# One store over 128 partitions in place of two over 64, in an attention and SoLU kernel

## The chip, the cores and the metric

The kernel runs on one core of one Trainium2 chip. The metric is the device time of one launch in microseconds; smaller is better. The core has five engines with a queue of instructions each: PE (TensorE, matrix products), ACT (ScalarE), DVE (VectorE), POOL (GpSimd) and SP (SyncE, which here only issues DMAs and waits). A DMA is issued by an engine's queue and carried out by the core's 16 DMA engines, which this document calls streams.

## What is computed

The reference, cut to what matters, takes q, k and v of shape (8, 8, 576, 64): eight batches, eight heads, 576 positions.

```python
kv  = np.einsum('bhsd,bhse->bhde', k, v)
o   = np.einsum('bhsd,bhde->bhse', q, kv)
x   = o / np.sqrt(np.mean(o * o, axis=-1, keepdims=True) + 1e-06) * g_norm   # heads side by side: 4608 x 512
h   = x @ w_in                                     # 4608 x 1024
solu = h * softmax(h)
ln  = (solu - mean(solu)) / np.sqrt(var(solu) + 1e-06) * g_ln
out = ln @ w_out                                   # 4608 x 512, float32
```

The result has 4608 rows of 512 float32 numbers, 9.44 MB.

## The kernel before

The 4608 rows are worked on in nine chunks of 512 rows. A position s of a batch is split as s = 9p + j, with p from 0 to 63 and j from 0 to 8. Chunk c of the first eight holds the positions with j from 0 to 7 of batch c; chunk 8 holds the positions with j = 8 of all eight batches.

For each chunk PE forms kv and o, ACT and DVE normalise o to x, PE forms h, ACT takes its exponential, DVE multiplies the two to u, and statistics of u give a factor `rstd` for each row. PE then forms u @ w_out, four tiles m = 0 to 3 of 128 rows into PSUM (`out_mm`, L608; its matmuls are line 612). For chunks 4 to 8 (`TOKEN_ROWS`) u has the rows on the partitions, and must be turned first: `u_turn` (L517) issues one DMA transpose for each m on SP's queue (line 519), and `out_mm` of that m waits for it. The q of chunks 5 to 8 (`Q_BY_DMA`) is turned by DMA on SP's queue too (`q_turn`, L301, line 304), and the chunk's o waits for that.

`scale` (L618) multiplies a PSUM tile by `rstd` into an SBUF tile `ob`. In chunks 0 to 7 two scaled tiles, m = yh and m = yh + 2, share one `ob` tile of 128 partitions by 2 x 512 numbers. `store_pair` (L634) then writes it out. On partition 64x + p stand the rows j = 2(2yh + x) and the next of position group p, and these are next to each other in memory: 1024 numbers, 4096 bytes. So each half of the partitions (x = 0, x = 1) goes with one DMA of 64 pieces of 4 KB, 256 KB in all, line 637. All sixteen of these pairs go by SP's queue. In chunk 8 a tile m holds two batches, 64 rows each; `store` (L645) writes each batch with one DMA of 64 pieces of 2 KB (line 647; m = 1 and 2 on ACT's queue, m = 0 on SP's). Its last tile, m = 3, is cut into two halves of 256 columns (`out_cols`, L649, matmuls on line 653; `scale_cols`, L655), and `store_cols` (L663) writes each with two DMAs of 64 pieces of 1 KB, line 666, the first half on SP's queue and the second on ACT's.

The order of all 844 pieces of work is written out by hand in `TABLE`, in one list for all engines; an engine takes its own pieces in that order and waits where an operand is not there. The same table gives each tile its place in memory, and places of `ob` tiles are used again by later tiles once the store has read them. Read from the table, SP issues from its first store on, with S(c, yh) for a pair of stores, uT(c, m) for a turn of u and qT(c) for a turn of q:

S(1,0), S(2,0), qT(5), qT(7), S(1,1), qT(6), uT(4,0), uT(4,3), uT(4,1), qT(8), S(3,0), S(3,1), uT(4,2), uT(5,0), uT(5,1), S(4,1), uT(5,3), uT(5,2), S(2,1), uT(6,0), uT(6,1), S(0,1), S(4,0), uT(6,2), uT(6,3), S(0,0), uT(7,0), uT(7,2), uT(7,1), S(5,1), uT(7,3), uT(8,1), S(6,1), S(5,0), uT(8,2), uT(8,0), uT(8,3), S(6,0), S(7,1), S(7,0), then the first tile and the first half-tile of chunk 8.

A turn of u moves 128 x 1024 two-byte numbers, 256 KB. The inputs are loaded by POOL's queue.

Of the kernel before, what the change touches and what calls it, by code (L numbers as in the profile page):

```python
# [102 lines left out]
def kernel(  # L103
# [11 lines left out]
    nc = tc.nc  # L115
    B, H, S, D = q.shape
    n_tok, d_model = out.shape
# [4 lines left out]
    NC = B + 1  # L122
# [7 lines left out]
    T = {}  # L130
# [144 lines left out]
    def kv_copy(engine, b, g, x, part):  # L275
        t = T["P", "kv", b, g, x]
        if b < 2:
            copy(engine, kvd[:, b, x, g], t[:, :, :])
        elif part == 0:
            copy(engine, kvd[:, b, x, x], t[:, :, :])  # L280
        else:
            z = part - 1
            copy(engine, kvd[z * 64:z * 64 + 64, b, 1 - x, x], t[(1 - z) * 64:(1 - z) * 64 + 64, :, :])
# [84 lines left out]
    for c in range(NC):  # L368
        if c < B:
            for g in halves(c):  # L370
                plan.add(("kv_mm", c, g), "pe", lambda _, c=c, g=g: kv_mm(c, g), [("k", c, g), ("v", c, g)],
                         uses=[("L", "k", c), ("L", "v", c)], first=[("P", "kv", c, g, x) for x in range(2)])
                for x in range(2):
                    for part in range(1 if c < 2 else 3):
                        plan.add(("kv", c, g, x, part), ("dve", "act"),
                                 lambda e, c=c, g=g, x=x, part=part: kv_copy(e, c, g, x, part),
# [5 lines left out]
        for hf in range(2):  # L382
            mine = [loads[hf]] if c < 2 else loads
            qT, qT_key = (("qT", c), ("L", "qT", c)) if c in Q_BY_DMA else (("qT", c, hf), ("S", "qT", c, hf))
            if c not in Q_BY_DMA:
                plan.add(("qT_mm", c, hf), "pe", lambda _, c=c, hf=hf: qT_mm(c, hf), ["ident", *mine], uses=quse,
                         first=[("P", "qT", c, hf)])
# [6 lines left out]
            for z in range(2):  # L394
                i = (c, hf, z)
                plan.add(("sq", i), "act", lambda _, i=i: o_sq(*i), [("o_mm", c, hf)], uses=[("P", "o", *i)],
                         first=[("S", "osq", *i)])
                plan.add(("s_mm", i), "pe", lambda _, i=i: s_mm(*i), [("sq", i)], uses=[("S", "osq", *i)],
                         first=[("P", "s", *i)])
                if c == 0:  # L400
                    plan.add(("ex", i), "act", lambda _, i=i: s_rsqrt(*i), [("s_mm", i)], uses=[("P", "s", *i)],
                             first=[("S", "rst", *i)])
                else:
                    plan.add(("ln", i), "act", lambda _, i=i: s_ln(*i), [("s_mm", i), "table"], uses=[("P", "s", *i)],
                             first=[("S", "lss", *i)])
                    plan.add(("ex", i), "act", lambda _, i=i: s_exp(*i), [("ln", i)], uses=[("S", "lss", *i)],
                             first=[("S", "rst", *i)])
                plan.add(("x", i), "dve", lambda _, i=i: x_mul(*i), [("ex", i)], after=[("x", (c, hf, 0))] if z else [],
                         uses=[("P", "o", *i), ("S", "rst", *i)] + ([("S", "x", c, hf)] if z else []),
                         first=[] if z else [("S", "x", c, hf)])  # L410
# [126 lines left out]
    for c in range(NC):  # L537
        xs = [[("x", (c, hf, z)) for z in range(2)] for hf in range(2)]
        if c not in TOKEN_ROWS:
            for f in range(NF):  # L540
                n_parts = h_parts(c)
                for part in range(n_parts):
# [4 lines left out]
                             first=[] if part else [("P", "h", c, f)],  # L547
# [5 lines left out]
                         first=[] if f % 2 else [("S", "u", c, f // 2)])  # L553
# [3 lines left out]
                         first=[] if f % 2 else [("S", "usq", c, f // 2)])  # L557
                if f % 2:
                    n = f // 2
# [3 lines left out]
                             first=[] if n % 2 else [("S", "es", c, n // 2)])  # L563
            for part, kind in enumerate(("u", "usq", "es")):
# [4 lines left out]
                         first=[] if part else [("P", "sum", c)])  # L569
            plan.add(("stats", c), "dve", lambda _, c=c: stats(c), [("sums", c, 2)], uses=[("P", "sum", c)])  # L570
        else:
            for m in range(4):
                for s in range(2):
# [7 lines left out]
                             first=[] if s else [("S", "u", c, m)])  # L581
# [33 lines left out]
    def paired(c):  # L615
        return c < B
# [15 lines left out]
    QUEUES = {"sp": nc.sync, "act": nc.scalar, "pool": nc.gpsimd}  # L632

    def store_pair(engine, c, yh):  # L634
        for x in range(2):
            j = 2 * (2 * yh + x)
            QUEUES[engine].dma_start(
                out[c * S:c * S + S, :].rearrange("(p j) d -> p (j d)", j=9)[:, j * d_model:(j + 2) * d_model],
                T["L", "ob", c, yh][64 * x:64 * x + 64].rearrange("p z d -> p (z d)"),
            )  # L640

    def rows_of(z, y):
        return out.rearrange("(b p j) d -> j b p d", p=64, j=9)[8, 2 * y + z]

    def store(engine, c, m):  # L645
        for x in range(2):
            QUEUES[engine].dma_start(rows_of(m // 2, 2 * (m % 2) + x), T["S", "ob", c, m][64 * x:64 * x + 64, :])  # L647

    def out_cols(x):  # L649
        cols = slice(x * d_model // 2, (x + 1) * d_model // 2)  # L650
# [11 lines left out]

    def store_cols(x):  # L663
        cols = slice(x * d_model // 2, (x + 1) * d_model // 2)
        for y in range(2):
            (nc.sync, nc.scalar)[x].dma_start(
                rows_of(1, 2 + y)[:, cols], T["S", "ob", NC - 1, 3, x][64 * y:64 * y + 64, :]
            )

    for half in range(2):  # L670
        plan.add(("w_mean", half), "pe", lambda _, half=half: w_mean(half), [("w_out", half), "g_mean"], after=[("w_mean", 0)] if half else [],
# [3 lines left out]
    for c in range(NC):  # L675
        last = c == NC - 1
        if c in TOKEN_ROWS:
            u_need = lambda m, half, c=c: [("uT", c, m)]
            u_use = lambda m, c=c: [("S", "uT", c, m)]
        else:  # L680
            u_need = lambda m, half, c=c: [("u", c, f) for f in range(4 * half, 4 * half + 4)]
            u_use = lambda m, c=c: [("S", "u", c, n) for n in range(NF // 2)]
        for m in range(3 if last else 4):
            for half in range(2):
                plan.add(("out", c, m, half), "pe", lambda _, c=c, m=m, half=half: out_mm(c, m, half),
                         [("w_center", f) for f in range(4 * half, 4 * half + 4)] + u_need(m, half), after=[("out", c, m, 0)] if half else [],
                         uses=u_use(m) + ([("P", "acc", c, m)] if half else []), first=[] if half else [("P", "acc", c, m)])
            plan.add(("ob", c, m), ("dve", "act"), lambda e, c=c, m=m: scale(e, c, m), [("out", c, m, 1), ("rstd", c)],
                     uses=[("P", "acc", c, m)] + ([("L", "ob", c, m % 2)] if paired(c) and m > 1 else []),
                     first=[("S", "ob", c, m)] if not paired(c) else [] if m > 1 else [("L", "ob", c, m)],  # L690
                     after=[("ob", c, m - 2)] if paired(c) and m > 1 else [])
            if last:
                plan.add(("store", c, m), ("sp", "act"), lambda e, c=c, m=m: store(e, c, m), [("ob", c, m)], uses=[("S", "ob", c, m)])
            elif m > 1:
                plan.add(("store", c, m - 2), "sp", lambda e, c=c, m=m: store_pair(e, c, m - 2),
                         [("ob", c, m), ("ob", c, m - 2)], uses=[("L", "ob", c, m - 2)])
        for x in range(2 if last else 0):
            plan.add(("out", c, 3, x), "pe", lambda _, x=x: out_cols(x),
                     [("w_center", f) for f in range(NF)] + u_need(3, 0) + u_need(3, 1), uses=u_use(3),
                     first=[("P", "acc", c, 3, x)])  # L700
            plan.add(("ob", c, 3, x), ("dve", "act")[x], lambda _, x=x: scale_cols(x), [("out", c, 3, x), ("rstd", c)],
                     uses=[("P", "acc", c, 3, x)], first=[("S", "ob", c, 3, x)])
            plan.add(("store", c, 3, x), ("sp", "act")[x], lambda _, x=x: store_cols(x), [("ob", c, 3, x)],
                     uses=[("S", "ob", c, 3, x)])
# [32 lines left out]
```

## Time and profile before

| What | Value |
|---|---|
| time, median of 3 runs | 186.5 us (186.12 to 187.28) |
| profiled execution, its own time | 186.57 us |
| its span, first to last instruction | 184.8 us |
| PE busy | 169.9 us, 92% of the span |
| ACT, DVE, POOL busy | 138.4, 123.2, 70.7 us |
| bytes moved by DMA | 34.60 MB, of these 9.44 MB written to memory |
| queue q1 (SP's DMAs) | 33264 packets, 16.33 MB |
| queue q0 (POOL's loads) | 15936 packets, 17.30 MB |
| queue q10 (ACT's DMAs) | 480 packets, 0.66 MB |

The time is 1.8 us more than the span, and the profiled execution lies 0.07 us above the median. A view of DMAs gives for each queue the packets, the megabytes, and the time that the packets took as a share of 16 streams. Its issue lines give how many DMAs a line issued, the size of one, and the median time from issue to landing. The view of stretches of time (windows) gives each engine's busy time with the number of instructions, the granted PE clock, the DMA share of 16 streams and the GB/s. A row of the timeline has start, duration, engine, line, operation, tiles and count; an engine with a q behind its name issues DMAs.

### The profile page before, as it was taken

What the parts mean: (1) busy time and instruction counts of PE and PEld (TensorE: products, weight loads), DVE (VectorE), ACT (ScalarE), POOL (GpSimd) and SP (SyncE); (2) the same over time, 40 slices, a digit from 0 to 9 for tenths busy, and PEclk for the clock granted to TensorE, in tenths of its full rate; (3) what the DMA queues carried; (4) which work ended last, traced back from release to release, by engine and by line L of the source; (5) the groups of instructions that cost most, each with busy time, mean ns of one, the idle gap of its engine ahead of it and who ended that gap; (6) DMA issues with size and microseconds to landing.
All of it is one profiled execution on the core that took longest, in us unless ns stands there. A gap on an engine that the chain in (4) does not pass through costs nothing.

```text
span 184.8 us, 4941 instructions
## 1 busy us (share of the span) xinstructions
PE 169.9 (92%) x1959; PEld 83.7 (45%) x1981; DVE 123.2 (67%) x294; ACT 138.4 (75%) x327; POOL 70.7 (38%) x105
## 2 busy tenths in 40 slices
PE   7979599979999999999999999999999999999950
PEld 2445344545445545464554444445444444344430
DVE  1011857798666675478666998888779978869430
ACT  2045878967798768986858999998899888877410
POOL 7953028697999068657950000001100300102000
PEclk9999999999999999999999999999999999999995
DMA  3999999999999999999799785650999966889975
GB/s 43 183 206 203 207 280 291 167 188 196 202 199 207 211 204 248 222 203 204 137 242 230 155 173 125 164 114 14 196 194 246 153 170 32 206 183 244 249 238 163
DMA packets 49703, 34.60 MB, mean 187 GB/s; under 512 B 32648, under 2 KB 46224, under 8 KB 49680
## 3 DMA queue, kind: packets, MB, share of 16 engines
q0 software_dynamic: 15936, 17.30, 54.3%
q1 hardware_dynamic: 33264, 16.33, 40.3%
q10 hardware_dynamic: 480, 0.66, 1.2%
q8 instruction: 15, 0.25, 0.5%
q14 instruction: 8, 0.07, 0.1%
HBM read 32.51 MB, written 9.44 MB: 227 GB/s over the span
## 4 chain that ended last, share of the span: by engine, by line
PE 73%; DMA 11%; ACT 7%; issue 2%; ACTq 2%; POOL 2%; DVE 0%; DVEq 0%; POOLq 0%
PE acc_ps L612 30%; PE h_ps L487 16%; PE h_ps L421 11%; DMA k_sb<-in_k_dram 8%; PE s_ps L341 4%; PE kv_ps L270 4%; PE o_ps L327 3%; DMA uT_sb<-u_sb 3%; PE sum_ps L459 2%; ACT osq_sb L176 2%; PE warm_ps L204 2%; ACT rst_sb L176 2%; ACTq L647 2%; PE qT_ps L293 1%; ACT e_sb L176 1%
## 5 line engine op out<-in xcount | busy, mean ns | idle before, releaser
L176 ACT ACTIVATE e_sb<-h_ps 128x512 f32<-128x512 f32 x72 | 42.1, 599 | 6.6 <-PE h_ps L421 3.1
L487 PE MATMUL h_ps<-w_in_sb,x_sb 128*128 128x512 bf16 x156 | 37.3, 379 | 0.3 <-issue 0.2
L612 PE MATMUL acc_ps<-w_out_sb,uT_sb 128*128 128x512 bf16 x147 | 35.9, 379 | 0.6 <-DMA uT_sb<-u_sb 0.3
L363 DVE SCALAR_TENSOR_TENSOR x_sb<-o_ps,g_rep,rst_sb 128x512 bf16<-128x512 f32 x36 | 26.0, 747 | 11.5 <-ACT rst_sb L176 11.2
L504 DVE SCALAR_TENSOR_TENSOR u_sb<-h_ps,e_sb 128x512 bf16<-128x512 f32 x40 | 26.9, 687 | 7.3 <-ACT e_sb L176 7.1
L612 PE MATMUL acc_ps<-w_out_sb,u_sb 128*128 128x512 bf16 x123 | 30.8, 379 | 0.2
L421 PE MATMUL h_ps<-x_sb,w_in_sb 128*128 128x512 bf16 x123 | 29.9, 379 | 0.4 <-issue 0.2
L447 POOL TENSOR_TENSOR es_sb<-e_sb 128x512 bf16<-128x512 f32 x16 | 20.3, 1275 | 21.1 <-ACT e_sb L176 18.6
L436 DVE TENSOR_TENSOR u_sb<-h_ps,e_sb 128x512 bf16<-128x512 f32 x32 | 21.3, 685 | 9.5 <-ACT e_sb L176 9.2
L525 POOL TENSOR_TENSOR both<-su 128x4 f32<-128x4 f32 x4 | 1.7, 422 | 65.6 <-DVE u_sb L504 65.6
L176 ACT ACTIVATE osq_sb<-o_ps 128x512 bf16<-128x512 f32 x36 | 20.6, 601 | 4.7 <-PE o_ps L327 4.6
L487 PEld LDWEIGHTS <-x_sb 128*128 128x128 bf16 x160 | 15.3, 98 | 18.4 <-issue 0.6
L176 ACT ACTIVATE lss_sb<-s_ps 128x512 f32<-128x512 f32 x32 | 19.1, 606 | 4.9 <-PE s_ps L341 4.5
L612 PEld LDWEIGHTS <-uT_sb 128*128 128x128 bf16 x152 | 14.5, 98 | 17.9 <-DMA uT_sb<-u_sb 0.8
L630 DVE TENSOR_SCALAR ob_sb<-acc_ps,rstd 128x512 f32<-128x512 f32 x22 | 16.2, 746 | 5.9 <-PE acc_ps L612 4.2
L176 ACT ACTIVATE rst_sb<-lss_sb 128x512 f32<-128x512 f32 x32 | 19.7, 636 | 0.3
L421 PEld LDWEIGHTS <-w_in_sb 128*128 128x128 bf16 x128 | 11.9, 98 | 14.6 <-issue 1.8
L612 PEld LDWEIGHTS <-u_sb 128*128 128x128 bf16 x128 | 12.1, 98 | 14.3 <-DVE x_sb L363 0.3
L443 POOL TENSOR_TENSOR usq_sb<-u_sb 128x512 bf16<-128x512 bf16 x15 | 15.6, 1043 | 4.1 <-DVE u_sb L436 4.1
L515 DVE SCALAR_TENSOR_TENSOR e_sb<-u_sb 128x512 f32<-128x512 bf16 x25 | 16.9, 688 | 0.2
L341 PE MATMUL s_ps<-osq_sb,head_mean 128*128 128x512 bf16 x36 | 13.3, 379 | 2.4 <-ACT osq_sb L176 2.3
L176 ACT ACTIVATE ob_sb<-acc_ps,rstd 128x512 f32<-128x512 f32 (+1 forms) x14 | 9.4, 675 | 5.7 <-DMA out_dram<-ob_sb 5.6
(80 smaller groups left out, 186.0 us busy)
## 6 DMA issues: line engine op xcount, KB each, us to landing
out_dram<-ob_sb SPq DMA_DIRECT2D x32, 256.0 KB, 3.7
q_sb<-in_q_dram POOLq DMA_DIRECT2D x6, 576.0 KB, 11.8
v_sb<-in_v_dram POOLq DMA_DIRECT2D x6, 576.0 KB, 11.5
k_sb<-in_k_dram POOLq DMA_DIRECT2D x6, 576.0 KB, 10.8
w_out_f<-in_moe_w_out_dram POOLq DMA_DIRECT2D x2, 1024.0 KB, 10.1
v_sb<-in_v_dram POOLq DMA_DIRECT2D x4, 288.0 KB, 8.2
k_sb<-in_k_dram POOLq DMA_DIRECT2D x4, 288.0 KB, 8.9
q_sb<-in_q_dram POOLq DMA_DIRECT2D x4, 256.0 KB, 9.0
```

Of the source, the lines that this page charges most:

```text
L176: nc.scalar.activation(out=dst, in_=src, func=func, **more)
L341: nc.tensor.matmul(t[:, :], head_mean[:, :], T[("S", "osq", *i)][:, :], start=True, stop=True)
L363: nc.vector.scalar_tensor_tensor(out=dst, in0=T["P", "o", c, hf, z].rearrange("p a b c -> p a (b c)"), scalar=g_rep[:, :], in1=T["S", "rst ...
L421: nc.tensor.matmul(T["P", "h", c, f][:, :], w_in_sb[:, dt, f * 128:(f + 1) * 128], flat(T["S", "x", c, dt // 2][:, dt % 2]), start=(dt == ...
L436: nc.vector.tensor_tensor(out=half_of("u", c, f), in0=T["P", "h", c, f][:, :], in1=T["S", "e", c, f][:, :], op=MUL)
L443: nc.gpsimd.tensor_tensor(out=dst, in0=src, in1=src, op=MUL)
L447: (nc.gpsimd if engine == "pool" else nc.vector).tensor_tensor(out=dst, in0=T["S", "e", c, 2 * n][:, :], in1=T["S", "e", c, 2 * n + 1][:, ...
L487: nc.tensor.matmul(t[:, :], T["S", "x", c, dt // 2][:, dt % 2, z, y:y + 2, :].rearrange("p y c -> p (y c)"), w_in_sb[:, dt, 512 * s:512 * ...
L504: nc.vector.scalar_tensor_tensor(out=T["S", "u", c, m][:, s, :], in0=T["P", "h", c, m, s][:, :], scalar=1.0, in1=T["S", "e", c, m, s][:, : ...
L515: nc.vector.scalar_tensor_tensor(out=dst, in0=src, scalar=1.0, in1=src, op0=MUL, op1=MUL, accum_out=acc)
L612: nc.tensor.matmul(T["P", "acc", c, m][:, :], u_cols(c, m, f), w_out_sb[:, f, :], start=(f == 0), stop=(f == NF - 1))
L630: nc.vector.tensor_scalar_mul(out=dst, in0=src, scalar1=by)
```

## The change

Each `ob` tile of 128 partitions is written by one DMA in place of two over 64 partitions each. The destination is written as a pattern of two blocks (step 4096 bytes within the row group for a pair, two batches for chunk 8) of 64 pieces; the source is the whole tile. The pieces keep their sizes of 4, 2 and 1 KB, the queues and the table stay as they are. SP then issues 16 pair stores in place of 32, and chunk 8 has five stores in place of ten.

```diff
     def store_pair(engine, c, yh):
-        for x in range(2):
-            j = 2 * (2 * yh + x)
-            QUEUES[engine].dma_start(
-                out[c * S:c * S + S, :].rearrange("(p j) d -> p (j d)", j=9)[:, j * d_model:(j + 2) * d_model],
-                T["L", "ob", c, yh][64 * x:64 * x + 64].rearrange("p z d -> p (z d)"),
-            )
-
-    def rows_of(z, y):
-        return out.rearrange("(b p j) d -> j b p d", p=64, j=9)[8, 2 * y + z]
+        QUEUES[engine].dma_start(
+            out[c * S:c * S + S, :].rearrange("(p j) d -> p (j d)", j=9)[:, 4 * yh * d_model:4 * (yh + 1) * d_model]
+            .rearrange("p (y n) -> y p n", y=2),
+            T["L", "ob", c, yh].rearrange("p z d -> p (z d)"),
+        )
+
+
+    def last_rows(m):
+        first = 4 * (m % 2) + m // 2
+        return out.rearrange("(b p j) d -> j b p d", p=64, j=9)[8, first:first + 3:2]
 
     def store(engine, c, m):
-        for x in range(2):
-            QUEUES[engine].dma_start(rows_of(m // 2, 2 * (m % 2) + x), T["S", "ob", c, m][64 * x:64 * x + 64, :])
+        QUEUES[engine].dma_start(last_rows(m), T["S", "ob", c, m][:, :])
...
     def store_cols(x):
         cols = slice(x * d_model // 2, (x + 1) * d_model // 2)
-        for y in range(2):
-            (nc.sync, nc.scalar)[x].dma_start(
-                rows_of(1, 2 + y)[:, cols], T["S", "ob", NC - 1, 3, x][64 * y:64 * y + 64, :]
-            )
+        (nc.sync, nc.scalar)[x].dma_start(last_rows(3)[:, :, cols], T["S", "ob", NC - 1, 3, x][:, :])
```

## The prediction

> **What bounds the kernel now.** I read the page's chain of work first, then the issue lines of the DMA view, then the DMA view of short stretches, and last SP's timeline.
>
> ```profile
> span 184.8 us, 4941 instructions
> PE 73%; DMA 11%; ACT 7%; issue 2%; ACTq 2%; POOL 2%; DVE 0%; DVEq 0%; POOLq 0%
> ```
>
> PE carries the end: 73% of the chain. DMA has 11% of it. The stores are off it until the last microseconds; what PE does wait for is turned data that comes through the same queue as the stores. So the stores are free only as long as they do not hold up the turns behind them on SP's queue.
>
> ```profile
> out_dram<-ob_sb SPq DMA_DIRECT2D x32, 256.0 KB, 3.7
> ...
> uT_sb<-u_sb SPq DMA_TRANSPOSE x20, 3.1
> ...
> out_dram<-ob_sb SPq DMA_DIRECT2D x2, 64.0 KB, 2.2
> ...
> g_rows<-in_moe_g_ln_dram SPq DMA_DIRECT2D x1, 4.0 KB
> ```
>
> A store of 256 KB lands in 3.7 us, a turn of u in 3.1 us. The reader should notice the last row: the load of `g_rows` (8 rows of 512 bytes, line 151) is the one group without a time to landing, and the view prints that time only when it counts 16 completions for each DMA. The DMA view of two stretches shows why. First, 4.6 to 6.5 us, where only the `g_rows` load runs on q1; then 148.0 to 150.4 us, where q1 moves the two halves of S(0,0).
>
> ```profile
> q1 hardware_dynamic: 16, 0.00, 1.3%
> ```
>
> ```profile
> q1 hardware_dynamic: 160, 0.52, 84.8%
> ```
>
> The load of 8 rows made 16 packets: 8 of data, and so 8 for completion. The two stores of 64 pieces made 160: 128 of data, and so 16 for completion each. A completion packet comes from each stream that takes part. So the number of streams is not always 16: it was 8 for a pattern whose slowest count is 8, and 16 for one whose slowest count is 64.
>
> **The change, part by part.** *Streams.* This decides everything. The tile side of the new store still counts 128 partitions slowest, but the memory side now counts 2 blocks slowest, then 64 pieces. If both sides are cut along their slowest count, as the 8-row load suggests, there are 2 equal parts, and 2 streams carry the whole store. The trace of before has no DMA whose memory side alone starts with so small a count, so it does not show this. Bounds: 16 streams (nothing changes but the issues) and 2 streams. I take 2, because the 8-row load is the nearest row in kind: it is the only small slowest count, and it held its DMA to that count.
>
> The Trainium skill's page "DMA: Bandwidth & Descriptors", section "Why a DMA increments its semaphore by 16 and not by 1", states that the number of engines is the largest one up to 16 that divides the slowest non-1 count of both sides, on this path the lowest-numbered ones. By that, the sum is the one below; the 8 completions of `g_rows` agree with it, and no run here yet shows it for a memory side of 2.
>
> *One pair store.* It moves 512 KB, so 262,144 bytes by each of 2 streams. What a stream moves is read from the view of stretches as GB/s over 16 times the share. The first row is the stretch in which streams moved most, the second one in which all were full of stores:
>
> ```profile
> 174.90:175.20 0.30, 0.30 (x3) 0.18 (x2) 0.30 (x2) 0.00 (x0) 0.00 (x0) 1.00 0.99 396
> 148.00:149.00 1.00, 1.00 (x6) 0.49 (x5) 0.95 (x3) 1.00 (x4) 0.00 (x0) 1.00 0.98 201
> ```
>
> 396 / (0.99 x 16) = 25.0 GB/s, so 10.5 us for a pair; 201 / (0.98 x 16) = 12.8 GB/s, so 20.5 us. I take 25.0, since two busy streams press on memory far less than 16; 12.8 stays as the upper bound. The same 25.0 GB/s gives 131,072 / 25.0 = 5.2 us for a tile of chunk 8 and 2.6 us for a half-tile.
>
> *What stands behind it.* A turn also goes through SP's queue and uses all streams, these two among them, so a turn behind a store waits for it. Its own share of the queue I take as the time of its issue: 1.26 us for a turn of u, 3.27 us for qT(5) to qT(7), 1.82 us for qT(8).
>
> ```profile
> L519 SPq DMA_TRANSPOSE uT_sb<-u_sb x20: 1231/1260/2462, 102.4 to 170.0; - x20
> ```
>
> ```profile
> L304 SPq DMA_TRANSPOSE qT_sb<-q_sb x3: 2072/3272/3489, 90.7 to 97.6; - x3
> L304 SPq DMA_TRANSPOSE qT_sb<-q_last x1: 1817/1817/1817, 106.5 to 106.5; - x1
> ```
>
> SP's timeline of before gives the order; a row joins neighbours of one kind:
>
> ```profile
> 68.68 21.79 SPq L637 DMA_DIRECT2D out_dram<-ob_sb  x4
> 90.70 5.53 SPq L304 DMA_TRANSPOSE qT_sb<-q_sb  x2
> 96.33 1.18 SPq L637 DMA_DIRECT2D out_dram<-ob_sb  x2
> 97.61 3.49 SPq L304 DMA_TRANSPOSE qT_sb<-q_sb  x1
> 102.42 3.94 SPq L519 DMA_TRANSPOSE uT_sb<-u_sb  x3
> 106.53 1.82 SPq L304 DMA_TRANSPOSE qT_sb<-q_last  x1
> 111.74 2.95 SPq L637 DMA_DIRECT2D out_dram<-ob_sb  x4
> 114.78 8.55 SPq L519 DMA_TRANSPOSE uT_sb<-u_sb  x3
> 128.09 1.11 SPq L637 DMA_DIRECT2D out_dram<-ob_sb  x2
> 129.29 3.73 SPq L519 DMA_TRANSPOSE uT_sb<-u_sb  x2
> 133.08 1.22 SPq L637 DMA_DIRECT2D out_dram<-ob_sb  x2
> 134.54 3.63 SPq L519 DMA_TRANSPOSE uT_sb<-u_sb  x2
> 138.22 3.09 SPq L637 DMA_DIRECT2D out_dram<-ob_sb  x4
> 141.41 5.31 SPq L519 DMA_TRANSPOSE uT_sb<-u_sb  x2
> 146.77 1.23 SPq L637 DMA_DIRECT2D out_dram<-ob_sb  x2
> 149.95 8.05 SPq L519 DMA_TRANSPOSE uT_sb<-u_sb  x3
> 158.05 1.23 SPq L637 DMA_DIRECT2D out_dram<-ob_sb  x2
> 160.29 2.91 SPq L519 DMA_TRANSPOSE uT_sb<-u_sb  x2
> 163.74 2.65 SPq L637 DMA_DIRECT2D out_dram<-ob_sb  x4
> 167.25 4.02 SPq L519 DMA_TRANSPOSE uT_sb<-u_sb  x3
> 171.36 8.08 SPq L637 DMA_DIRECT2D out_dram<-ob_sb  x6
> 179.54 1.38 SPq L647 DMA_DIRECT2D out_dram<-ob_sb  x2
> 181.01 1.23 SPq L666 DMA_DIRECT2D out_dram<-ob_sb  x2
> ```
>
> S(1,0), issued at 68.7 us, costs nothing even at 20.5 us: the next DMA of this queue, S(2,0), goes out just ahead of 90.5 us (68.68 + 21.79). If that cover were gone, the walk would start up to 10.5 us later. From 90.5 us I walk the two streams: S(2,0) to 101.0; qT(5) and qT(7) to 107.5; S(1,1) to 118.0; qT(6) to 121.3, which before was issued at 97.6, so PE now waits for o of chunk 6 some 18 us; three turns of u to 125.1; qT(8) to 126.9; S(3,0) and S(3,1) to 147.9; uT(4,2) to 149.2. Here is the one place where the queue runs dry by my reading: S(4,1) needs the product of chunk 4 that waits for uT(4,2). Before, uT(4,2) went out at 114.8, landed about 3.1 us later (117.9), and S(4,1) followed at 128.1, 10.2 us after. So S(4,1) starts at 159.4, and uT(5,0) and uT(5,1) fill only 2.5 of these 10.2 us: 7.7 us idle. Elsewhere what the next DMA needs is made while the queue is still busy: the turn that it rests on lies at least one store, 10.5 us, earlier.
>
> On from 159.4: S(4,1) 169.9, two turns 172.4, S(2,1) 182.9, two turns 185.4, S(0,1) and S(4,0) 206.4, two turns 208.9, S(0,0) 219.4, three turns 223.2, S(5,1) 233.7, two turns 236.2, S(6,1) and S(5,0) 257.2, three turns 261.0, S(6,0), S(7,1) and S(7,0) 292.5. Then chunk 8: three tiles, 15.7 us, and two half-tiles, 5.2 us, to 313.4. ACT's queue issues three of these five, but onto the same two streams, so they add up all the same. As a sum: 90.5 + 15 x 10.5 + 11.6 (four turns of q) + 20 x 1.26 + 7.7 + 20.9 = 313.4. About 2 us to the end of the span (a 64 KB store lands in 2.2 us), and the 1.8 us by which the profiled execution's 186.57 us exceeds its span: 317 us. That execution stands at the median, so nothing is added for it.
>
> *Issues.* 21 stores instead of 42 are issued, saving SP and ACT about half a microsecond for each (1.11 us for the two at 128.09); that is hidden behind the streams and I cost it at nothing. *Places of `ob`.* A store lands some 8 us later, so a later `ob` tile in its place waits (ob(3,0) uses that of S(2,0)); the queue is full by more than that, so nothing is added.
>
> **The rivals.** *A, not slower:* the 128 partitions decide alone, and 16 streams run as before. Then only issues go, which counts at the end:
>
> ```profile
> 175.29 3.06 ACTq L647 DMA_DIRECT2D out_dram<-ob_sb  x4
> ...
> 178.46 0.47 ACT L176 ACTIVATE ob_sb<-acc_ps,rstd 128x256 f32<-128x256 f32 x1 [5.59 <-DMA out_dram<-ob_sb]
> 178.96 1.71 ACTq L666 DMA_DIRECT2D out_dram<-ob_sb  x2
> ```
>
> ACT issues four stores for 3.06 us ahead of its last scale, and two after it for 1.71. With half of them, up to 1.5 + 0.9 = 2.4 us go, less what PE then holds back: about 2 us, 184.5 us. It decides if a store leaves 16 completion packets. For it: 64 and 128 both divide by 16, and nothing measured has a small count on the memory side alone. Against it: the 8-row load.
>
> The Trainium skill speaks for A as well: the same page, section "Rules for kernel authors", advises one 128-partition transfer instead of two over disjoint halves, as these share the engines anyway. By that alone the sum would be A's 184.5 us. The two halves of S(0,0) on q1 above agree that both use 16 streams.
>
> *B:* 2 streams, but another pair for each store. Then stores overlap one another and the turns are held up by one store at most; what remains is the tail, where a half-tile takes 2.6 us instead of a fraction, and a turn late by up to 10.5 us once or twice: about 200 us. For it speaks nothing in the trace, against it nothing either.
>
> *C:* 2 streams, the same pair, but turns do not stand behind stores. Then the streams still carry all stores: 313.4 - 36.8 (turns) - 7.7 = 268.9, plus 3.8: 273 us. Against it: both are on q1.
>
> **How the numbers follow.** My forecast, 2 streams with turns behind, has 0.79, B 0.05, C 0.06. A stream as slow as 12.8 GB/s would add 15 x 10.0 + 20 = 170 us, 487 us; I give that and other slow mixtures 0.03, since 16 full streams are not there. A has 0.07. The forecast's own range and C's together give 273 at the low end; the high end of 370 is a stream at about 19 GB/s, between the two bounds (13.8 us a pair, 15 x 3.3 + 6.6 = 56 more). Low end and high end leave out A, B and the slow mixture, 0.15, and a little of the forecast. Within 1% is about what a measurement of this kernel can tell from no change. Faster by over 1% is A where it gains its full 2 us, 0.05; within 1%, A where it gains less, 0.02; slower all else, 0.93.
>
> **What would show it.** For the streams: a pair store leaves 2 completion packets instead of 32, so its stretch shows 130 packets on q1, and the store lines lose their time to landing as `g_rows` did. For the price: the GB/s of slices late in the span fall to about 50, two streams of 25. For the turns: PE waits for uT and qT by 10 to 20 us at a time, and these turns land 10 us and more after issue. For the idle place: a stretch without store packets between uT(5,1) and S(4,1). Wrong would be: 16 completions for each store (A), turns that land in 3 us beside slow stores (C), or a pair that takes clearly more or less than 10.5 us.

## The result, and the profile after

The changed kernel takes 324.4 us (median of 4 runs, 323.15 to 325.38) against 186.6 us (186.12 to 187.28): a ratio of 1.738, with a 95% interval of 1.730 to 1.746. The forecast was 317 us in a range of 273 to 370.

The first lines of the page after, with the chain of work:

```profile
span 323.6 us, 4940 instructions
...
DMA  6999999999991996491319942949793914111111
GB/s 100 204 206 303 184 200 202 209 209 221 166 49 43 149 61 161 101 68 53 85 10 60 97 79 58 68 98 51 111 64 81 68 53 106 52 52 52 52 51 42
...
DMA 37%; PE 29%; SPq 9%; ACT 4%; POOL 4%; issue 1%; DVE 1%; DVEq 0%; ACTq 0%; POOLq 0%
DMA uT_sb<-u_sb 33%; PE acc_ps L612 14%; SPq L304 9%; PE h_ps L421 6%; DMA k_sb<-in_k_dram 4%; POOL es_sb L447 2%; PE s_ps L341 2%; PE kv_ps L270 2%; PE h_ps L487 2%; POOL usq_sb L443 1%; ACT osq_sb L176 1%; ACT e_sb L176 1%; PE warm_ps L204 1%; ACT rst_sb L176 1%; PE o_ps L327 1%
```

PE had 73% of the chain before and has 29% now; DMA has 37%, nearly all of it turns of u, which is what PE now waits for. The GB/s line ends in a row of 52 and less: in the last six slices of 8.1 us stores are all that the streams carry, at no more than 52 GB/s. The view of stretches and the DMA view, both of 300 to 310 us, say how many streams that is:

```profile
300.00:310.00 10.00, 0.00 (x0) 0.00 (x0) 0.00 (x0) 0.00 (x0) 0.00 (x0) 0.50 0.13 52
```

```profile
q1 hardware_dynamic: 88, 0.36, 8.7%
q10 hardware_dynamic: 88, 0.16, 4.2%
```

All five engines are idle, and the DMA share is 0.13: 2 of 16 streams (0.125). SP's and ACT's queues share them, 8.7% and 4.2%. 52 / 2 = 26 GB/s for each stream. The issue lines after have lost their times to landing:

```profile
out_dram<-ob_sb SPq DMA_DIRECT2D x16, 512.0 KB
...
uT_sb<-u_sb SPq DMA_TRANSPOSE x20
```

as the 8-row load had none before. (The turns lose theirs too; why was not looked into.) The count of packets settles the number. Before, a tile's two stores left 160 packets on q1; SP issues 18 such tiles. If a tile is now stored in k streams it leaves 128 + k, so q1 falls from 33264 by 18 x (32 - k). The line of the page after:

```profile
q1 hardware_dynamic: 32724, 16.33, 54.3%
```

33264 - 32724 = 540 = 18 x 30, so k = 2. SP's timeline after, where it answers to the walk:

```profile
68.19 21.21 SPq L635 DMA_DIRECT2D out_dram<-ob_sb  x2
89.65 21.73 SPq L304 DMA_TRANSPOSE qT_sb<-q_sb  x2
111.43 0.52 SPq L635 DMA_DIRECT2D out_dram<-ob_sb  x1
...
130.82 1.54 SPq L635 DMA_DIRECT2D out_dram<-ob_sb  x2
132.46 23.36 SPq L519 DMA_TRANSPOSE uT_sb<-u_sb  x3
167.12 0.51 SPq L635 DMA_DIRECT2D out_dram<-ob_sb  x1
167.73 12.20 SPq L519 DMA_TRANSPOSE uT_sb<-u_sb  x2
179.98 0.51 SPq L635 DMA_DIRECT2D out_dram<-ob_sb  x1
...
268.76 11.34 SPq L635 DMA_DIRECT2D out_dram<-ob_sb  x3
280.20 14.72 SPq L647 DMA_DIRECT2D out_dram<-ob_sb  x1
295.03 14.11 SPq L665 DMA_DIRECT2D out_dram<-ob_sb  x1
```

Line 635 is the new pair store, 665 the new half-tile. A turn behind a store now holds SP while it is issued: three turns that follow S(3,0) and S(3,1) take 23.36 us, where 1.26 us was a turn's issue before. In the view of waits, PE's sum over turns of u shows what that does:

```profile
PE acc_ps L612 <- DMA uT_sb<-u_sb: 67.3, 8, 17.0
```

Eight waits, the longest of 17.0 us. In the chain the turns of u have 33% of 323.6 us, 107 us.

### The profile page after: what moved, and what is told of

Read it like the earlier page. It is cut to its first block, busy times and chain, and to the rows that moved or that the text cites. A ratio compares the mean times of both kernels' runs of the same rounds, so it can differ in the third digit from the quotient of the medians.

```text
span 323.6 us, 4940 instructions
## 1 busy us (share of the span) xinstructions
PE 191.8 (59%) x1981; PEld 87.8 (27%) x1981; DVE 123.6 (38%) x294; ACT 139.5 (43%) x327; POOL 70.6 (22%) x105
## 3 DMA queue, kind: packets, MB, share of 16 engines
q1 hardware_dynamic: 32724, 16.33, 54.3%
q0 software_dynamic: 15936, 17.30, 30.9%
## 4 chain that ended last, share of the span: by engine, by line
DMA 37%; PE 29%; SPq 9%; ACT 4%; POOL 4%; issue 1%; DVE 1%; DVEq 0%; ACTq 0%; POOLq 0%
DMA uT_sb<-u_sb 33%; PE acc_ps L612 14%; SPq L304 9%; PE h_ps L421 6%; DMA k_sb<-in_k_dram 4%; POOL es_sb L447 2%; PE s_ps L341 2%; PE kv_ps L270 2%; PE h_ps L487 2%; POOL usq_sb L443 1%; ACT osq_sb L176 1%; ACT e_sb L176 1%; PE warm_ps L204 1%; ACT rst_sb L176 1%; PE o_ps L327 1%
## 5 line engine op out<-in xcount | busy, mean ns | idle before, releaser
L612 PE MATMUL acc_ps<-w_out_sb,uT_sb 128*128 128x512 bf16 x152 | 49.2, 479 | 67.3 <-DMA uT_sb<-u_sb 67.3
L487 PE MATMUL h_ps<-w_in_sb,x_sb 128*128 128x512 bf16 x160 | 43.3, 419 | 11.0 <-issue 11.0
L612 PEld LDWEIGHTS <-uT_sb 128*128 128x128 bf16 x152 | 17.1, 118 | 95.3 <-DMA uT_sb<-u_sb 70.6
L487 PEld LDWEIGHTS <-x_sb 128*128 128x128 bf16 x160 | 16.5, 106 | 33.7 <-issue 19.1
L341 PE MATMUL s_ps<-osq_sb,head_mean 128*128 128x512 bf16 x36 | 14.5, 414 | 2.2 <-ACT osq_sb L176 2.1
```

The lines of the kernel that those rows point to most:

```text
L341: nc.tensor.matmul(t[:, :], head_mean[:, :], T[("S", "osq", *i)][:, :], start=True, stop=True)
L487: nc.tensor.matmul(t[:, :], T["S", "x", c, dt // 2][:, dt % 2, z, y:y + 2, :].rearrange("p y c -> p (y c)"), w_in_sb[:, dt, 512 * s:512 * ...
L612: nc.tensor.matmul(T["P", "acc", c, m][:, :], u_cols(c, m, f), w_out_sb[:, f, :], start=(f == 0), stop=(f == NF - 1))
```

## The experiments

Two theories were put against each other. The *streams theory*: the slowest count of the memory side sets how many streams carry a store, and two are too few. The *size theory*: one DMA of 512 KB over 128 partitions is slow, or blocks its queue, whatever its pattern. For the first I needed other counts on the memory side. A pair's 128 rows have no single step in memory, but 128 rows over two neighbouring batches do (9 rows), so several kernels below store to those. What they leave out is the right place of the rows; bytes, piece length and row pitch are kept.

**One uniform DMA.**

```diff
-            out[c * S:c * S + S, :].rearrange("(p j) d -> p (j d)", j=9)[:, 4 * yh * d_model:4 * (yh + 1) * d_model]
-            .rearrange("p (y n) -> y p n", y=2),
+            out[c // 2 * 2 * S:(c // 2 + 1) * 2 * S, :].rearrange("(p j) d -> p (j d)", j=9)
+            [:, (2 * (c % 2) + yh) * 2 * d_model:(2 * (c % 2) + yh + 1) * 2 * d_model],
...
-        return out.rearrange("(b p j) d -> j b p d", p=64, j=9)[8, first:first + 3:2]
+        return out.rearrange("(p j) d -> j p d", j=9)[8, 128 * m:128 * m + 128]
```

> One DMA over 128 partitions for each store, as in the changed kernel, but its memory side counts 128 pieces of 4 KB at one step (two neighbouring batches), so no slowest count of 2; sizes, piece lengths and row pitch are kept. The rows of the result land in other places than the reference's. Streams theory (the slowest count of the memory side sets the number of streams): 16 streams, 128 + 16 = 144 packets on q1 for a pair store, and rival A's price, 184.5 us (183 to 186). Size theory (one DMA of 512 KB over 128 partitions is slow by itself, or holds up the queue by its size): about 320 us as in the changed kernel.

Measured: 182.7 us (181.91 to 183.31), ratio 0.978 (0.975 to 0.982) to the kernel before on the same chip, a little below the 183 to 186 expected. The q1 line of its page:

```profile
q1 hardware_dynamic: 32976, 16.33, 35.0%
```

33264 - 32976 = 288 = 18 x 16: 16 streams. The size theory falls: the same number of DMAs of the same size gains 4.1 us instead of losing 138.

**Two DMAs over 64 partitions, each with a slowest count of 2.**

```diff
-                out[...].rearrange("(p j) d -> p (j d)", j=9)[:, j * d_model:(j + 2) * d_model],
+                out[...].rearrange("(p j) d -> p (j d)", j=9)[:, j * d_model:(j + 2) * d_model]
+                .rearrange("(p y) n -> y p n", y=2),
```

> Two DMAs over 64 partitions for each store as in the kernel before, but each memory side is written as 2 blocks (every other row) of 32 pieces. The rows of the result land in other places than the reference's. Streams theory: 2 streams for each, 32 x 4 KB by each stream, so 10.5 us for the two halves together at 25.0 GB/s and a time like the changed kernel's, 315 to 330 us. Size theory: DMAs of the old size and number, so 186 us.

Measured: 344.7 us (one run). The old number and size of DMAs is as slow as the new one when the memory side counts 2 slowest. Its page has 32760 packets on q1, and 33264 - 32760 = 504 = 36 x 14: two streams for each of SP's 36 stores. It is 20 us slower than the changed kernel and above the 330 that I gave. SP's timeline has 14 of these 20 us between S(4,1) and S(6,0), 170.4 to 286.4 us, 116.0 us where the changed kernel takes 101.6; why two DMAs on two streams cost more than one was not settled.

**2, 4, 8 and 16 blocks.** The uniform store's rows, counted as K blocks of every K-th row:

```diff
-            [:, (2 * (c % 2) + yh) * 2 * d_model:(2 * (c % 2) + yh + 1) * 2 * d_model],
+            [:, (2 * (c % 2) + yh) * 2 * d_model:(2 * (c % 2) + yh + 1) * 2 * d_model].rearrange("(p y) n -> y p n", y=K),
...
-        return out.rearrange("(p j) d -> j p d", j=9)[8, 128 * m:128 * m + 128]
+        return out.rearrange("(p j) d -> j p d", j=9)[8, 128 * m:128 * m + 128].rearrange("(p y) d -> y p d", y=K)
```

> As the runs with 4, 8 and 16 blocks, with 2 blocks of 64 pieces: the control that ties that series to the changed kernel. The rows of the result land in other places than the reference's. Streams theory: 2 streams, 324 us (318 to 332) like the changed kernel. If the placing of the rows matters by itself: away from 324 us by more than 8 us.

> As the run with one uniform DMA, but the 128 pieces are counted as 4 blocks of 32 (every fourth row). The rows of the result land in other places than the reference's. Streams theory: 4 streams, 131072 / 25.0 = 5.2 us for a pair; the queue from 90.5 us on holds 15 x 5.2 + 11.6 + 25.2 + some 8 idle + 10.5 = 134 us, so 228 us (215 to 245). Size theory: 320 us. If any small count were equally bad: 320 us.

> As before, with 8 blocks of 16. The rows of the result land in other places than the reference's. Streams theory: 8 streams, 2.6 us for a pair; the queue's load from 90.5 us on is 39 + 37 + 5 = 81 us, less than the 94 us that the kernel before took from there, so turns are late by a few us only: 186 to 200 us. Size theory: 320 us.

> As the runs with 4 and 8 blocks, with 16 blocks of 8 pieces. The rows of the result land in other places than the reference's. Streams theory: 16 streams, so as the uniform store, 182.7 us (181.5 to 184). If what the changed pattern costs is that neighbouring pieces lie further apart in memory (every 16th row here, more than with 2, 4 or 8 blocks): slower than the 214.9 us of 8 blocks.

Measured, with the q1 packets of each page and the k worked out from them:

| K | time, us | q1 packets | 33264 less this | k |
|---|---|---|---|---|
| 2 | 324.5 (one run) | 32724 | 540 = 18 x 30 | 2 |
| 4 | 260.3 (one run) | 32760 | 504 = 18 x 28 | 4 |
| 8 | 214.9 (one run) | 32832 | 432 = 18 x 24 | 8 |
| 16 | 184.0 (182.52 to 184.44), ratio 0.983 (0.979 to 0.987) | 32976 | 288 = 18 x 16 | 16 |

The number of streams is the slowest count, at each value, and the time follows it; with 2 blocks the time is that of the changed kernel within 0.1 us, though its rows lie elsewhere. The Trainium skill's rule (page "DMA: Bandwidth & Descriptors", section "Why a DMA increments its semaphore by 16 and not by 1") agrees with all four counts.

With 4 blocks the time is 32 us above the 228 that I expected, with 8 it is 15 us above the upper end of 200. The view of stretches of the run with 4 blocks shows where. The columns are, at the end of a row, PE clock, DMA share and GB/s:

```profile
151.50:155.50 4.00, 4.00 (x27) 1.71 (x24) 3.58 (x9) 2.84 (x10) 0.00 (x0) 1.00 0.23 47
155.50:156.50 1.00, 0.23 (x8) 0.00 (x0) 0.64 (x3) 1.00 (x4) 0.00 (x0) 1.00 0.25 102
```

Both stretches have four streams busy (0.23 and 0.25 of 16) and move nothing but a store's packets. In the second they move 102 GB/s, 25 for each, as I took; in the first 47. The first lies while a turn stands begun behind the store. In these 4 us the store loses 4 x (1 - 47 / 102) = 2.2 us, and if every store lost as much, 15 stores would make 32 us. SP's issues bear that out as a mean: from S(4,1) at 148.8 us to S(6,0) at 226.5 us lie eight pairs and fourteen turns, 77.8 us, where 8 x 5.2 + 14 x 1.26 = 59.2 us were expected, so 2.3 us more for each pair. So a store on few streams and a turn slow each other, which my walk did not have. What makes them do so was not tried by itself.

**Only the pairs, and only chunk 8.** The first kernel has the new `store_pair` alone, the second the new chunk 8 alone.

```diff
-            QUEUES[engine].dma_start(
-                out[...].rearrange("(p j) d -> p (j d)", j=9)[:, j * d_model:(j + 2) * d_model],
...
+            .rearrange("p (y n) -> y p n", y=2),
+            T["L", "ob", c, yh].rearrange("p z d -> p (z d)"),
```

```diff
-            QUEUES[engine].dma_start(rows_of(m // 2, 2 * (m % 2) + x), T["S", "ob", c, m][64 * x:64 * x + 64, :])
+        QUEUES[engine].dma_start(last_rows(m), T["S", "ob", c, m][:, :])
```

> Only the sixteen pair stores are changed; chunk 8 is stored by two DMAs over 64 partitions as before. Streams theory: the walk without chunk 8's 20.9 us on two streams and with about 3 us in their place, 317 - 18 = 299 us, or 306 us with the 7 us by which the changed kernel exceeded the walk. If chunk 8's stores carried the loss: near 200 us.

> Only chunk 8's five stores are changed. Streams theory: 15.7 + 5.2 us on two streams from about 176 us on, then 2 us to the end of the span and 1.8 us beside it: 201 us (195 to 205). If two streams are slow only because many stores queue up: no more than 190 us.

Measured: 307.7 us and 203.7 us (one run each). The view of stretches of the second, behind the last product:

```profile
180.00:198.00 18.00, 0.00 (x0) 0.00 (x0) 0.00 (x0) 0.00 (x0) 0.00 (x0) 0.50 0.13 48
```

Eighteen microseconds in which nothing runs but two streams. Both times are as expected from the streams theory. Over 186.5 us the parts cost 121.2 and 17.2 us, in sum 138.4, and both together 137.8.

**The pair stores on POOL's queue.**

```diff
-        QUEUES[engine].dma_start(
+        nc.gpsimd.dma_start(
...
-                plan.add(("store", c, m - 2), "sp", ...
+                plan.add(("store", c, m - 2), "pool", ...
```

> The changed kernel, but the sixteen pair stores are issued by POOL's queue, so that no turn stands behind one in SP's queue. Theory that the turns lose because they stand behind stores in one queue, with stores on the same two streams: turns land sooner, the sum of stores still fills two streams, about 273 to 300 us. If stores of this queue take another pair of streams each time (rival B): about 190 to 215 us. If the queue does not matter: 324 us.

Measured: 281.7 us (one run), in the first theory's range, but not for its reason alone. Queue q0 and the issue lines of its DMA view:

```profile
q0 software_dynamic: 32576, 25.75, 55.1%
...
out_dram<-ob_sb POOLq DMA_DIRECT2D x16, 512.0 KB, 18.6
...
uT_sb<-u_sb SPq DMA_TRANSPOSE x20, 14.8
```

A pair's store lands 18.6 us after issue and a turn 14.8, against 3.1 before, though no turn stands behind a pair in its queue. So leaving the queue is worth 43 us of 138, and most of the loss stays. My reading, which this run does not show turn by turn, is that a turn needs all the streams and meets the store on some of them. POOL's own work stands behind the waits of the stores there; it has 2% of the chain, and the run does not take it apart. The view of stretches has, at a place where only store packets run:

```profile
199.00:203.00 4.00, 4.00 (x23) 1.68 (x21) 3.39 (x10) 2.93 (x10) 0.00 (x0) 1.00 0.23 69
```

A share of 0.23 is 3.7 streams, more than two, so two stores ran side by side on different pairs: rival B's condition, at least in part.

**A layout that allows 16 streams, in chunk 8 alone.** A tile of chunk 8 takes two neighbouring batches.

```diff
-            tile_of(("S", "x", c, hf), [128, 2, 2, 4, 64], BF16)
+            tile_of(("S", "x", c, hf), [128, 2, 4, 2, 64] if c == B else [128, 2, 2, 4, 64], BF16)
...
+            return x[:, m].rearrange("p z c -> p (z c)") if c == B else x[:, z, y:y + 2, :].rearrange("p y c -> p (y c)")
...
+        return out.rearrange("(p j) d -> j p d", j=9)[8, 128 * m:128 * m + 128]
```

> The kernel before, with pair stores of 64 partitions as they were; in chunk 8 a tile holds two neighbouring batches in place of two that lie apart (x of chunk 8 is laid out with the parity inside), so that its 128 rows have one step in memory and one DMA stores them in 16 streams. It computes the reference's result. Streams theory and the price of issues: ACT issues two stores in place of four ahead of its last scale (3.06 us before), one in place of two behind it: 184.5 us, 1% faster. If the end is set by something else than the issues: 186.5 us.

Measured: 185.9 us (184.48 to 187.02), ratio 0.997 (0.994 to 1.000): no difference that can be told. Timelines of its end, and of the uniform store's:

```profile
175.37 1.68 ACTq L656 DMA_DIRECT2D out_dram<-ob_sb  x2
...
177.68 2.03 ACTq L674 DMA_DIRECT2D out_dram<-ob_sb  x1
```

```profile
174.26 1.00 ACTq L646 DMA_DIRECT2D out_dram<-ob_sb  x2
...
176.57 0.34 ACTq L664 DMA_DIRECT2D out_dram<-ob_sb  x1
```

Ahead of the last scale ACT's issues fell from 3.06 to 1.68 us, as expected. But the one store behind it took 2.03 us to issue, more than the two of before (1.71). ACT is done with it at 179.7 us, before at 180.7, and of that 1 us the span keeps 0.6 (184.2 against 184.8). In the uniform kernel, where the pairs are single stores too, the last issue took 0.34; why it is slower here was not looked into.

**The same for pairs: o interleaved.** Pairs get a slowest count of 64 when the partitions hold position group p and block x in the order 2p + x. PE puts o into that order, first by how it reads q, in the second kernel by how it writes to PSUM (its lines are against the first); chunk 8 is as in the run above.

```diff
+            .rearrange("p (y n) -> p y n", y=2),                             # the store's memory side
...
+                            dst = dst.rearrange("p y c -> p (y c)").rearrange("p (h c x) -> p h c x", h=2, x=2)
+                            src = src.rearrange("p (h x) c -> p h c x", x=2)
```

```diff
-                            dst = dst.rearrange("p y c -> p (y c)").rearrange("p (h c x) -> p h c x", h=2, x=2)
-                            src = src.rearrange("p (h x) c -> p h c x", x=2)
+                            dst = dst.rearrange("p y c -> p (y c)").rearrange("p (h c x) -> p h x c", h=2, x=2)
+                            src = src.rearrange("p (h x) c -> p h x c", x=2)
```

> A kernel that computes the reference's result and stores each pair by one DMA in 16 streams: o is written to PSUM with the two row blocks of a pair interleaved, so that on partition 2p + x stand the rows of position group p, and the memory side counts 64 groups, then 2 blocks, then 1024 numbers; chunk 8 holds neighbouring batches in a tile as in the run before. Streams theory: slowest counts 64 and 128, 16 streams, 144 packets for a pair, and the uniform store's time, 182.7 us, 2% faster than the kernel before. If the small count anywhere in the pattern costs, or the interleaved o costs PE more: 186 us or more.

> As the run with the interleaved o, which computes the reference's result and whose products of o took 402 ns in place of 269: here PE reads q in its own order, at one step, and interleaves as it writes to PSUM. If reading at a wide step cost the 133 ns, they are 269 ns again, and the time is the uniform store's, 182.7 us (182 to 184). If writing every other number costs it: 402 ns and 186.3 us as in the run before.

Measured: 186.3 us (185.42 to 186.95), ratio 0.998 (0.996 to 1.000), and 185.4 us (184.11 to 186.52), ratio 0.995 (0.992 to 0.998). Both store in 16 streams (32976 packets on q1). The products of o, in the kernel before and in these two:

```profile
L327 PE MATMUL o_ps<-qT_sb,kvd x192: 192/269/293, 11.9 to 150.7; 64*64 64x256 bf16 x128, 64*64 64x64 bf16 x64
```

```profile
L331 PE MATMUL o_ps<-qT_sb,kvd x192: 192/402/425, 11.9 to 153.6; 64*64 64x256 bf16 x128, 64*64 64x64 bf16 x64
```

```profile
L331 PE MATMUL o_ps<-qT_sb,kvd x192: 192/400/418, 11.6 to 153.3; 64*64 64x256 bf16 x128, 64*64 64x64 bf16 x64
```

The medians of 269, 402 and 400 ns are of products over 256 and over 64 columns together. Grouped by form, the 64-column products stay at a mean of 195 ns, and those over 256 columns go from 279 to 411 and 410 ns; PE is busy with the latter for 10.3 and 9.4 us in place of 6.0. The last o starts 2.6 to 2.9 us later (150.7 before, 153.3 and 153.6). Of the 4.1 us that the uniform store gains, 0.4 and 1.0 us are left. The 4.3 and 3.4 us of added work on PE are of the size of what is missing; no run has the interleaving without the joined stores. The second is the fastest of the kernels here that leave nothing out, half a per cent ahead of the kernel before the change.

## Why the prediction was right, step by step

*Two streams* was right. It rested on the 8-row load and its 8 completions; the series from 2 to 16 blocks shows it.

*10.5 us for a pair* was right for a pair alone: 26 GB/s for a stream in the tail against 25.0 taken, which makes 10.1 us.

*Turns stand behind stores*: the walk, against the times at which SP issued the store.

| | walk, us | after, us | difference |
|---|---|---|---|
| S(1,1) | 107.5 | 111.4 | 3.9 |
| S(3,0) | 126.9 | 130.8 | 3.9 |
| S(4,1), behind the idle place | 159.4 | 167.1 | 7.7 |
| S(2,1) | 172.4 | 180.0 | 7.6 |
| S(6,0) | 261.0 | 268.8 | 7.8 |
| end of the span | 315.4 | 323.6 | 8.2 |

From S(4,1) to S(6,0), eight pairs and fourteen turns, the walk has 101.6 us and the profile 101.6. That they agree to the tenth is luck in part: at the tail's 52 GB/s the eight pairs have 8 x 10.1 = 80.8 us of it, and the turns, with what they hold up, 20.8 us where the walk has 17.6. A pair taken as too slow made up for turns taken as too cheap. The 8 us that were missing came at two places.

The first is S(2,0) with two turns of q, 3.9 us. The DMA view of 92.8 to 106.9 us, in which S(2,0) ran, and the issue line of the loads of `q_last`:

```profile
q1 hardware_dynamic: 128, 0.52, 9.7%
q0 software_dynamic: 126, 0.09, 4.1%
```

```profile
q_last<-in_q_dram POOLq DMA_DIRECT2D x2, 64.0 KB, 22.2
```

The pair took 14.1 us, not 10.5, while POOL's last loads were still on the streams: the two shares make 13.8%, about two of 16 streams (12.5%), and the load of `q_last` landed after 22.2 us, before after 10.0. I had walked the queue of SP alone and left q0 out. Two smaller errors nearly cancel: the pair's first packets come at 92.8 us and not 90.5, and the two turns behind it take 4.5 us (106.9 to 111.4) and not 6.5. In sum 3.6 + 2.3 - 2.0 = 3.9.

The second is the idle place, 3.8 us. The chain of work puts the landing of uT(4,2) and its neighbours at 132.46 + 23.12:

```profile
132.46 23.12 DMA uT_sb<-u_sb
```

that is 155.6, and S(4,1) came 11.5 us later, not 10.2. Between the two no packet of a store runs, as forecast (the last of S(3,1) ends at 154.2 us, the first of S(4,1) starts at 168.3). The rest, some 2.5 us, lies ahead of the landing: S(3,0) is issued at 130.8 and its first packet runs at 132.6, as the turn ahead of it, which I had counted by its issue alone, is still moving; and the two pairs take 21.6 us (to 154.2), not 21.0. For the 1.3 us the view of stretches offers a reason:

```profile
142.00:155.00 13.00, 0.00 (x0) 0.00 (x0) 0.98 (x3) 0.00 (x0) 0.00 (x0) 0.59 1.12 68
155.60:162.60 7.00, 6.97 (x19) 2.58 (x20) 1.98 (x6) 2.92 (x6) 0.00 (x0) 0.58 0.22 49
```

PE idles for 13 us, and in the 7 us after it works at a granted clock of 0.58. At the full clock the same work would take up to 7.0 x 0.42 = 2.9 us less by estimate, so the clock is more than enough for the 1.3 us. The Trainium skill's page "TensorE: Matmul & The Clock Gate", section "Part 1: The HAM clock gate", warns of just this, a clock that halves when PE idles for some microseconds; this trace agrees. No run here takes the clock apart from the wait.

*Chunk 8* was put at 20.9 us on two streams; alone it cost 17.2 us of time, since a part of it takes the place of what was there before.

*Rival A* (16 streams) did not happen, but its price can be checked with the uniform store: 182.7 us where I had 184.5. I had counted the issues of chunk 8 and not those of the pairs, nor that a pair's transfer gets faster: S(0,0) moves at 357 GB/s in 147.30 to 148.77 us there, before at 238 GB/s in 148.00 to 150.20. Which of the two made the gain was not separated; with 16 blocks, where S(0,0) moves at 229 GB/s in 147.70 to 149.90, the ratio was 0.983 against the uniform 0.978. The Trainium skill's advice for one 128-partition transfer (page "DMA: Bandwidth & Descriptors", section "Rules for kernel authors") holds there, and in the changed kernel costs 138 us: it needs a slowest count that divides by 16 on both sides. *Rival C*'s condition was approached by POOL's queue: 281.7 us, near its 273, but with turns that were late all the same, which C had excluded. It met *rival B*'s condition better, and for that my 200 us was far too low: I had let a turn be late by up to 10.5 us once or twice, and the median turn landed 14.8 us after its issue.

## What to carry to other kernels

Before two stores are joined, write down the slowest count of both sides: with the powers of two tried here the smaller one, up to 16, is the number of streams, and the packets of completion in a profile tell it afterwards. A store that is slow by itself may be hidden; what it costs is read from what stands behind it in the same queue and on the same streams, here the turns that PE waits for. To win the issues of joined stores, the rows must lie at one step, or be counted by 16 or by 64 first (the two counts tried here), and the reordering that this takes is itself to be paid.

## What the runs showed of the hardware that was not expected

- A turn that meets a store on two of its streams stays in flight as a whole: after S(2,1), in 182 to 183 us of the changed kernel, the DMA share is 12.88, the sum of packets that then wait for microseconds:

```profile
182.00:183.00 1.00, 1.00 (x4) 0.34 (x3) 0.00 (x0) 0.00 (x0) 0.00 (x0) 0.50 12.88 149
183.00:186.00 3.00, 3.00 (x10) 1.14 (x9) 0.00 (x0) 0.67 (x2) 0.00 (x0) 0.60 0.13 34
```

  In the 3 us after, the two streams move 34 GB/s and not 52.
- Issuing a DMA is not always short: ACT's half-tile of chunk 8 took 13.45 us to issue behind two stores on the same two streams, and 0.34 us in the uniform kernel.

```profile
277.24 13.45 ACTq L665 DMA_DIRECT2D out_dram<-ob_sb  x1
```

- A store with a count of 2 on POOL's queue leaves 1040 packets, (32576 - 15936) / 16, not 130: 128 of data and 912 others.
- A product over 256 columns takes 411 or 410 ns on average instead of 279, whether it reads or writes them interleaved by two.
- S(0,0) stored over 128 partitions at one step moves at 357 GB/s, as two stores over 64 partitions at 238 and in 16 blocks at 229, all in 16 streams; why was not tried.
